# Weight differences of a seven-product scheme: made and split once, and read back by the later blocks

## The chip, the cores and the metric

The kernel runs on one core of a Trainium2 chip. The metric is the device time of one execution, in microseconds (us). The engines are TensorE (PE, with its weight loads shown as PEld), VectorE (DVE), ScalarE (ACT), GpSimd (POOL) and SyncE (SP), which issues most of the DMA transfers.

## The reference

A windowed attention gives 2304 tokens of 512 features. A small network (three products, their maximum, an output product) changes each token's features. Then follows a mixture of 8 experts, in which every token goes through every expert, weighted by a gate that is balanced over 8 rounds:

```python
for e in range(E):                      # E = 8
    h = np.maximum(x @ w1[e], 0.0)      # [2304, 512] @ [512, 1024]
    ye = h @ w2[e]                      # [2304, 1024] @ [1024, 512]
    out += P[:, e:e + 1] * ye
```

The change is in the mixture, in the product with `w2[e]`, "the second product".

## The kernel before

**Splits.** A product in full precision is made of three products of the type fp32r. Each operand X is split into a high part (`hi`: ACT casts X) and a low part (`lo`: X - hi, on POOL or DVE); the three are hi*hi, hi*lo and lo*hi (`PASS`, line 344). The helper `split` (lines 66 to 69) issues the cast (L68) and the subtraction (L69). All casts of all splits carry line 68, all subtractions line 69, so the profile is read by tile names: `wa` (pieces of w1), `wb` and `wt` (pieces of w2), `hop` and `h` (pieces of the hidden values).

**Seven products for eight.** A product of two matrices cut into 2x2 quarters is made of seven quarter products with sums of quarters (Winograd's form of Strassen's scheme). For the second product, with the quarters b11, b12, b21, b22 of a pair of row blocks of w2, the weights are B11, B21, B22 and four differences: T1 = b12 - b11, T2 = b22 - T1, T3 = b22 - b12, T4 = b21 - T2. On the side of the hidden values the sums are S1 to S4.

**Blocks.** The 2304 tokens go in three blocks of 768, each as two halves of 384.

**The first block** (lines 773 to 916) has 32 stages: 8 experts times 4 pairs of 128-wide pieces of the hidden layer. Only the first product uses the seven-product scheme here (matmuls at L788); the second one is done plainly, by `Before.tile` (L740), one stage behind. A stage fetches two raw weight tiles two stages ahead (`fetch_w2`, L527), makes the sums of w1's quarters on DVE (`sums_w2`, L537), splits A1, S12, S34 and A2 for the next stage (`split_w2`: ACT, POOL) and writes each split to a DRAM tensor `wsd` (L557), which the later blocks read. The raw tiles' part of w2 is split whole by `split_out` into `wb`. ACT, DVE and PE run in the order in which the code is written; the orders of POOL's and SP's work are chosen by the scheduler. In stages 0 to 5 the balancing of the gate (`sinkhorn`) is woven in: `next(gate, None)` issues a few small DVE steps or one small matmul (L717). PSUM banks `p` and `q` change roles: the copy of `u2` out of the bank (ACT, L861) must be done before S3's product adds to the same bank.

**The two later blocks** (lines 1034 to 1130) have 16 passes, one for each block and expert. A pass has two halves. The first half makes the hidden values with the first product (L1066, 168 matmuls of 384 columns), with weights read from `wsd` (L563). The second half makes the second product by the seven-product scheme: 28 units u = 7 products x 4 pairs, 9 matmuls of 256 columns each (L998, 252 matmuls). Class `Second` prepares it. `sums` (L950 to L955) makes T1 to T4 on DVE, four subtractions a pair, in place in the raw tile. `weight(u)` splits one weight (ACT cast, POOL subtraction) into a tile `wt`. `mix` (L972, L974) and `rows(u)` (L983 for S4, then the split into `hop`: ACT cast, DVE subtraction) make the other operand. `ready(k)` moves a finished product out of PSUM (L1011, L1016, L1025, L1027). In the second half the code has, for each unit,

```python
sec.product(u)
if u % NPAIR == NPAIR - 1: sec.ready(u // NPAIR)
if 2 * NPAIR <= u + 6 < len(units): sec.rows(u + 6)
if 3 * NPAIR <= u + 10 < len(units): sec.weight(u + 10)
```

so that a unit's `hop` is prepared six units ahead and its `wt` ten.

Of the kernel before, what the change touches and what calls it, by code (L numbers as in the profile page):

```python
# [9 lines left out]
F32 = mybir.dt.float32  # L10
F32R = mybir.dt.float32r
U32 = mybir.dt.uint32
AF = mybir.ActivationFunctionType
ALU = mybir.AluOpType
# [30 lines left out]
E, F2 = 8, 1024  # L45
P = 128
# [15 lines left out]
NPAIR = NF2 // 2  # L62
# [3 lines left out]
def split(nc, hi, lo, src, sub):  # L66

    nc.scalar.copy(hi, src)  # L68
    sub.tensor_tensor(out=lo, in0=src, in1=hi.bitcast(F32), op=ALU.subtract)  # L69
# [16 lines left out]
def attention_moe(ctx: ExitStack, tc: tile.TileContext, q, k, v, mask, wm1, wg, wm2, out):  # L86
    nc = tc.nc
# [15 lines left out]
    cx_p = tc.alloc_tile_pool(name="cx", bufs=3)  # L103
# [5 lines left out]
    xg_p = tc.alloc_tile_pool(name="xg", bufs=1)  # L109
# [162 lines left out]
    x2d = dram.tile([P, KT, NT], F32, name="x2d")  # L272
    x2s = dram.tile([P, 2, KT, NT], F32, name="x2s")
    x2t = dram.tile([4, P, 2, 2, HT], F32, name="x2t")
    wsd = dram.tile([E * NPAIR, 4, P, 2, 512], F32, name="wsd")
    x2 = {}

# [288 lines left out]
    def split_out(raws, i):  # L566
        t = wb2_p.tile([P, 2, 512], F32R, name="wb2")
        split(nc, t[:, 0], t[:, 1], raws[i][:, 1], nc.gpsimd)
        return t

    def fetch_x(blk, queue):
        xs = []
        for j in range(2):
            t = cx_p.tile([P, KT, HT], F32, name="xh", tag="cx")
            c = (2 * blk + j) * HT
            queue.dma_start(t, x2d[:, :, c:c + HT])
            xs.append(t)
        return xs
# [95 lines left out]
    h1_p.release()  # L674
    ps_g.release()
    wb2_p = tc.alloc_tile_pool(name="wb2", bufs=5, reuse_waits="tile")
    h2_p = tc.alloc_tile_pool(name="h2", bufs=2, reuse_waits="tile")
    cc_p = tc.alloc_tile_pool(name="cc", bufs=2, reuse_waits="tile")
    ac_p = tc.alloc_tile_pool(name="ac", bufs=8, reuse_waits="tile")
    sms_p = tc.alloc_tile_pool(name="sms", bufs=1, reuse_waits="tile")  # L680
    ps_c = tc.alloc_tile_pool(name="ps_c", bufs=1, space=PSUM, reuse_waits="tile")

# [90 lines left out]
    for i, (blk, e, n) in enumerate(stages):  # L773
# [49 lines left out]
        def more_x(name):  # L823
            if not last:
                return
            if name[0] == "B":
                load_x(blk + 1, name)
            else:
                split_x(x_ops[blk + 1], name, later_x, nc.gpsimd)
# [3 lines left out]
        def halves(f, j, c):  # L833
            h = hs[f, j]
            nc.scalar.activation(out=h[:, 0], in_=c, func=AF.Relu)
            nc.vector.scalar_tensor_tensor(
                out=h[:, 1], in0=c, scalar=0.0, in1=h[:, 0].bitcast(F32), op0=ALU.max, op1=ALU.subtract
            )
# [13 lines left out]
        product(q, "A12", "B21", True, True)  # L852
        plus(q, m1)
        halves(0, 0, m1)
        more_x("B21")
        sum_x(last or farther)
        second(1, 0)
# [43 lines left out]
        if i:  # L901
            next(gate, None)
        ws.append(split_out(raws, 1))
        more_x("T3")
        keep_x(3)
        keep_x(4)
# [2 lines left out]
        if i + 2 < len(stages):  # L909
            ahead_w[i + 2] = fetch_w2(*stages[i + 2][1:])  # L910
        before = Before((blk, e, n), hs, ws, po, acc)
    for what in UP:
        load_w2(len(stages) + 1, what)
    for j in (1, 0):
# [1 line left out]
            before.tile(j, t)  # L916


    for pool in (sms_p, ac_p, cc_p, h2_p, wb2_p, xg_p, cx_p, sm_p):
        pool.release()  # L920

    def pool(name, bufs=1):
# [14 lines left out]
    class Second:  # L937


        def __init__(self, blk, e, raws):  # L940
            self.blk, self.e, self.raws = blk, e, raws
            self.r, self.h, self.w, self.m, self.ps, self.t2, self.s2 = {}, {}, {}, {}, {}, {}, {}

        def quarters(self, n):
            return {(f, d): self.raws[n][:, f, d * 256:(d + 1) * 256] for f in range(2) for d in range(2)}

        def sums(self, n, last):
            b, sub = self.quarters(n), partial(nc.vector.tensor_tensor, op=ALU.subtract)
            if last:
                sub(out=b[0, 1], in0=b[1, 1], in1=b[0, 1])  # L950
                sub(out=b[1, 0], in0=b[1, 0], in1=self.t2[n])
            else:
                self.t2[n] = tmp_p.tile([P, 256], F32, name="t2", bufs=3)
                sub(out=b[0, 0], in0=b[0, 1], in1=b[0, 0])
                sub(out=self.t2[n], in0=b[1, 1], in1=b[0, 0])  # L955

        def weight(self, u):
            k, n = units[u]
            name = ORD[k][2]
            b = self.quarters(n)  # L960
            if name == "T2":
                src = self.t2[n]
            else:
                src = b[{"B11": (0, 0), "B21": (1, 0), "T1": (0, 0), "T3": (0, 1), "B22": (1, 1), "T4": (1, 0)}[name]]
            t = wt_p.tile([P, 2, 256], F32R, name=f"wt{k % 3}")
            split(nc, t[:, 0], t[:, 1], src, nc.gpsimd)
            self.w[u] = t

        def mix(self, n):
# [64 lines left out]
    for g in range((NBLK - 1) * E):  # L1034
        blk, e = 1 + g // E, g % E
        sec = Second(blk, e, outs.pop(g))
        for n0 in range(0, NPAIR, 2):
# [61 lines left out]
            for k in both:  # L1099
                product(k, 1, "S1", "T1", True)  # L1100
                keep(k, 1, "m1")
                sec.rows(n0 + k)
                sec.sums(n0 + k, False)
            later("S12")
            for k in both:
                product(k, 0, "S3", "T3", False)
                plus(k, 0, "m1", 1, 1)
                sec.sums(n0 + k, True)
            for k in both:
                product(k, 1, "S4", "B22", False)  # L1110
                plus(k, 1, "u2", 0, 1)
# [90 lines left out]
```

## Time and profile before

| what | value |
|---|---|
| median of 3 runs | 1986.23 us (1984.38 to 1986.75) |
| the profiled execution | 1987.47 us, span 1985.7 us, mean granted clock 0.992 |
| PE busy | 1905.0 us (96%) |
| DVE, ACT, POOL busy | 1290.7, 991.6, 837.5 us |
| attention, small network | 0 to about 428 us |
| first block | about 428 to 934 us, 32 stages |
| later blocks | about 934 to 1981 us, 16 passes of 65.5 us (64.7 for expert 0) |

The profiled execution's span runs from its first to its last instruction; its time is 1.8 us longer. Busy time of PE is that of modelled, overlapping matmuls, so what a stretch loses is read from the time between two marks in it, against the number of matmuls between them.

### The profile page before, as it was taken

How to read it: one execution, taken by the hardware profiler on the slowest of the kernel's cores; microseconds unless marked ns; L12 is line 12 of the kernel's file. 1: busy time of each engine (PE TensorE's matmuls, PEld its weight loads, DVE VectorE, ACT ScalarE, POOL GpSimd, SP SyncE). 2: the span in 40 equal slices, each digit the busy share in tenths (PEclk: the TensorE clock that was granted, in tenths of full speed). 3: DMA queues.
4: the chain of work that ended last, by engine and by line, in shares of the span. 5: the costliest groups of instructions: out<-in, count | busy, mean ns of one | idle time of the engine just before them, and what ended most of it. 6: DMA issues, size and time to landing. Idle time of an engine off the chain costs nothing.

```text
span 1985.7 us, 35177 instructions
## 1 busy us (share of the span) xinstructions
PE 1905.0 (96%) x12873; PEld 1800.2 (91%) x12873; DVE 1290.7 (65%) x2361; ACT 991.6 (50%) x2523; POOL 837.5 (42%) x795
## 2 busy tenths in 40 slices
PE   7889999999999999999999999999999999999998
PEld 6789999998889899998999999998999899989998
DVE  7983333437554444444877787778777877787778
ACT  5654453434434444443654565455645565556554
POOL 5673333434444464444433343234423442344233
PEclk7999999999999999999999999999999999999999
DMA  8644445354555575557455344534763346334530
GB/s 266 227 170 160 161 140 196 101 185 175 190 183 190 184 270 187 188 186 279 155 163 160 114 149 152 170 110 146 268 204 116 130 149 191 117 118 149 192 117 33
DMA packets 134861, 334.61 MB, mean 169 GB/s; under 512 B 12705, under 2 KB 58401, under 8 KB 133153
## 3 DMA queue, kind: packets, MB, share of 16 engines
q1 hardware_dynamic: 132000, 328.43, 48.8%
q10 hardware_dynamic: 2688, 3.93, 0.6%
q8 instruction: 102, 1.67, 0.3%
q14 instruction: 71, 0.57, 0.1%
HBM read 246.86 MB, written 85.46 MB: 167 GB/s over the span
## 4 chain that ended last, share of the span: by engine, by line
PE 66%; DVE 20%; ACT 7%; issue 4%; DMA 2%; SPq 0%; POOL 0%; ACTq 0%; DVEq 0%; POOLq 0%
PE po L740 12%; PE po L998 11%; PE ps L379 9%; PE po L1066 9%; DVE hop L69 6%; PE p L788 6%; PE q L788 5%; PE p L1066 4%; PE q L1066 4%; ACT hop L68 3%; PE ps L399 3%; DVE r L983 2%; DVE r L972 2%; ACT wt L68 2%; DVE s L974 1%
## 5 line engine op out<-in xcount | busy, mean ns | idle before, releaser
L998 PE MATMUL po<-wt,hop 128*128 128x256 f32 x4032 | 528.9, 287 | 38.9 <-ACT hop L68 17.2
L998 PEld LDWEIGHTS po<-wt,hop 128*128 128x128 f32 x4032 | 494.9, 191 | 72.3 <-DVE hop L69 28.6
L69 POOL TENSOR_TENSOR wt<-raw,wt 128x256 fp32r<-128x256 f32 x384 | 344.5, 919 | 432.1 <-ACT wt L68 428.1
L69 DVE TENSOR_TENSOR hop<-r,hop 128x384 fp32r<-128x384 f32 x384 | 249.9, 677 | 186.1 <-ACT hop L68 186.1
L740 PE MATMUL po<-wb,h 128*128 128x512 f32 x1152 | 294.5, 392 | 0.2 <-POOL wb L69 0.2
L68 ACT CAST hop<-r 128x384 fp32r<-128x384 f32 x384 | 190.7, 513 | 127.7 <-DVE r L983 127.7
L379 PE MATMUL ps<-xt,wa 128*128 128x288 f32 x1728 | 242.7, 299 | 5.3 <-DVE h L69 3.1
L740 PEld LDWEIGHTS po<-wb,h 128*128 128x128 f32 x1152 | 213.9, 188 | 33.7 <-POOL wb L69 0.7
L379 PEld LDWEIGHTS ps<-xt,wa 128*128 128x128 f32 x1728 | 233.2, 190 | 8.5 <-DVE h L69 3.6
L69 POOL TENSOR_TENSOR wa<-raw,wa 128x512 fp32r<-128x512 f32 x112 | 134.2, 1203 | 170.9 <-ACT wa L68 165.0
L1080 ACT ACTIVATE r<-r 128x384 f32<-128x384 f32 x192 | 100.8, 525 | 170.1 <-DVE r L1079 170.1
L1066 PE MATMUL po<-xT,wa 128*128 128x384 f32 x768 | 157.1, 339 | 0.0
L68 ACT CAST wt<-raw 128x256 fp32r<-128x256 f32 x384 | 155.0, 404 | 0.0
L69 POOL TENSOR_TENSOR wt<-t,wt 128x256 fp32r<-128x256 f32 x64 | 46.8, 740 | 220.7 <-ACT wt L68 220.7
L1066 PEld LDWEIGHTS po<-xT,wa 128*128 128x128 f32 x768 | 135.6, 188 | 2.0
L69 POOL TENSOR_TENSOR wa<-sums,wa 128x512 fp32r<-128x512 f32 x64 | 83.0, 1318 | 93.4 <-ACT wa L68 93.4
L1066 PE MATMUL po<-xB,wa 128*128 128x384 f32 x576 | 116.9, 338 | 0.0
L69 POOL TENSOR_TENSOR wb<-raw,wb 128x512 fp32r<-128x512 f32 x64 | 85.4, 1334 | 59.4 <-ACT wb L68 59.1
L972 DVE TENSOR_TENSOR r<-r,r 128x384 f32<-128x384 f32 x128 | 101.4, 792 | 2.2
L1066 PEld LDWEIGHTS po<-xB,wa 128*128 128x128 f32 x576 | 102.5, 188 | 0.0
L1066 PE MATMUL p<-xT,wa 128*128 128x384 f32 x384 | 79.7, 342 | 3.0 <-DVE r L1079 3.0
L788 PE MATMUL q<-xT,wa 128*128 128x384 f32 x384 | 78.2, 339 | 0.0
(187 smaller groups left out, 3072.0 us busy)
## 6 DMA issues: line engine op xcount, KB each, us to landing
wa<-wsd SPq DMA_DIRECT2D x192, 512.0 KB, 4.4
wsd<-wa SPq DMA_DIRECT2D x96, 512.0 KB, 2.7
raw<-in_wm SPq DMA_DIRECT2D x64, 512.0 KB, 3.6
raw<-in_wm SPq DMA_DIRECT2D x128, 256.0 KB, 2.9
wa<-wsd SPq DMA_DIRECT2D x64, 256.0 KB, 4.5
cx<-in_wm SPq DMA_DIRECT2D x12, 1024.0 KB, 7.1
raw<-wm1f SPq DMA_DIRECT2D x24, 512.0 KB, 3.4
qt<-in_q SPq DMA_DIRECT2D x16, 576.0 KB, 6.1
```

Of the source, the lines that this page charges most:

```text
L68: nc.scalar.copy(hi, src)
L69: sub.tensor_tensor(out=lo, in0=src, in1=hi.bitcast(F32), op=ALU.subtract)
L379: nc.tensor.matmul(ps, w[:, wi, kk], xt[:, xi, kk, n0:n0 + HB], start=(n == 0), stop=(n == 3 * KT - 1),)
L399: nc.tensor.matmul(ps, wo[f][:, wi, d2 * P:(d2 + 1) * P], hs[f][:, hi, a * HB:(a + 1) * HB], start=(f == 0 and n == 0), stop=(f == NF1 - 1 ...
L740: nc.tensor.matmul(po, self.hs[f, j][:, hi, t * P:(t + 1) * P], self.ws[f][:, wi], start=(n + f + k == 0), stop=(n == NPAIR - 1 and f == 1 ...
L788: nc.tensor.matmul(ps, wo[w][:, wi, kk], xo[x][:, xi, kk], start=(first and k == 0), stop=True if k == 5 else False, skip_group_check=not ...
L972: nc.vector.tensor_tensor(out=r[o, n], in0=r[x, n], in1=r[y, n], op=op)
L974: nc.vector.tensor_tensor(out=self.s2[n], in0=r[(1, 1), n], in1=r[(0, 0), n], op=ALU.subtract)
L983: nc.vector.tensor_tensor(out=r[(1, 0), n], in0=r[(1, 0), n], in1=self.s2[n], op=ALU.subtract)
L998: nc.tensor.matmul(self.ps[side, t][:, 0:256], h[:, hi, t * P:(t + 1) * P], w[:, wi], start=(first and i == 0), stop=(n == NPAIR - 1 and i ...
L1066: nc.tensor.matmul(ps[k][side], wo[k][w][:, wi, kk], xo[x][:, xi, kk], start=(first and c == 0), stop=c == 5, skip_group_check=not first,)
L1080: nc.scalar.activation(out=r, in_=r, func=AF.Relu)
```

## The change

The first block now makes T1 to T4 too, splits them and writes the splits to a new DRAM tensor `wtd`; the later blocks load them from there. B11, B21 and B22 are split in the later blocks as before.

- `sums_out`, at the end of each stage: four DVE subtractions on the two raw tiles into a tile `ts` (one buffer).
- `keep_out`, in the next stage behind `halves(0, 0, m1)`: two splits of 512 columns (ACT, POOL) into tiles `tw`, and four DMA writes of 256 KB on SP's queue. For the last stage it stands behind the loop.
- In `Second`, `sums` is gone, and `weight(u)` of a T weight is one DMA load of 256 KB on SP's queue into the same `wt` buffers, in the places where the splits were.
- `ts` and `tw` have a new pool; the pools `cc` and `ac` have 1 and 6 buffers for 2 and 8.

```diff
+    wtd = dram.tile([E * NPAIR, 4, P, 2, 256], F32, name="wtd")
...
+    def sums_out(raws):
+
+        s = wt_p.tile([P, 4, 256], F32, name="ts", bufs=1)
+        (b11, b12), (b21, b22) = ((r[:, 1, 0:256], r[:, 1, 256:512]) for r in raws)
+        for o, x, y in ((0, b12, b11), (1, b22, s[:, 0]), (2, b22, b12), (3, b21, s[:, 1])):
+            nc.vector.tensor_tensor(out=s[:, o], in0=x, in1=y, op=ALU.subtract)
+        return s
+
+    def keep_out(i, s):
+        for o in (0, 2):
+            t = wt_p.tile([P, 2, 512], F32R, name="tw")
+            split(nc, t[:, 0], t[:, 1], s[:, o:o + 2].rearrange("p o n -> p (o n)"), nc.gpsimd)
+            for k in range(2):
+                nc.sync.dma_start(wtd[i, o + k], t[:, :, k * 256:(k + 1) * 256].bitcast(F32))
...
+    wt_p = tc.alloc_tile_pool(name="wto", bufs=2, reuse_waits="tile")
     h2_p = tc.alloc_tile_pool(name="h2", bufs=2, reuse_waits="tile")
-    cc_p = tc.alloc_tile_pool(name="cc", bufs=2, reuse_waits="tile")
-    ac_p = tc.alloc_tile_pool(name="ac", bufs=8, reuse_waits="tile")
+    cc_p = tc.alloc_tile_pool(name="cc", bufs=1, reuse_waits="tile")
+    ac_p = tc.alloc_tile_pool(name="ac", bufs=6, reuse_waits="tile")
...
         halves(0, 0, m1)
+        if i:
+            keep_out(i - 1, ts)
         more_x("B21")
...
         ws.append(split_out(raws, 1))
+        ts = sums_out(raws)
         more_x("T3")
...
+    keep_out(len(stages) - 1, ts)
...
-        def sums(self, n, last):
-            b, sub = self.quarters(n), partial(nc.vector.tensor_tensor, op=ALU.subtract)
...
         def weight(self, u):
             k, n = units[u]
             name = ORD[k][2]
-            b = self.quarters(n)
-            if name == "T2":
-                src = self.t2[n]
+            t = wt_p.tile([P, 2, 256], F32R, name=f"wt{k % 3}")
+            if name[0] == "T":
+                nc.sync.dma_start(t.bitcast(F32), wtd[self.e * NPAIR + n, int(name[1]) - 1])
             else:
-                src = b[{"B11": (0, 0), "B21": (1, 0), "T1": (0, 0), "T3": (0, 1), "B22": (1, 1), "T4": (1, 0)}[name]]
-            t = wt_p.tile([P, 2, 256], F32R, name=f"wt{k % 3}")
-            split(nc, t[:, 0], t[:, 1], src, nc.gpsimd)
+                f, d = int(name[1]) - 1, int(name[2]) - 1
+                split(nc, t[:, 0], t[:, 1], self.raws[n][:, f, d * 256:(d + 1) * 256], nc.gpsimd)
             self.w[u] = t
...
                 sec.rows(n0 + k)
-                sec.sums(n0 + k, False)
...
                 plus(k, 0, "m1", 1, 1)
-                sec.sums(n0 + k, True)
```

## Rows read from the trace of the kernel before

**Rows 1.** Page, part 1: busy us, share of the span, instructions
```profile
PE 1905.0 (96%) x12873; PEld 1800.2 (91%) x12873; DVE 1290.7 (65%) x2361; ACT 991.6 (50%) x2523; POOL 837.5 (42%) x795
```

**Rows 2.** Windows (length; busy PE, PEld, DVE, ACT, POOL; clock; DMA share; GB/s): block, pass, half
```profile
430.00:937.00 507.00, 504.58 (x2523) 453.78 (x2522) 250.88 (x476) 211.22 (x431) 242.96 (x196) 1.00 0.57 203
1003.00:1068.50 65.50, 62.83 (x422) 60.26 (x421) 50.73 (x94) 36.02 (x93) 24.50 (x28) 1.00 0.46 145
1029.20:1064.60 35.40, 32.91 (x254) 30.80 (x253) 29.98 (x51) 19.22 (x53) 16.25 (x18) 1.00 0.27 88
```

**Rows 3.** Chain that ended last, in order of time: start us, us, what
```profile
1029.28 8.65 PE po L998 x72
...
1064.68 1.06 PE q L1066 x6
...
1094.78 8.64 PE po L998 x72
```

**Rows 4.** Timeline of PE: start us, us, instruction, idle before and releaser
```profile
1026.82 1.32 PE L1066 MATMUL p<-xT,wa 128*128 128x384 f32 x6 [0.19 <-DVE r L1079]
...
1044.66 9.73 PE L998 MATMUL po<-wt,hop 128*128 128x256 f32 x79 [0.69 <-DVE hop L69]
...
1056.80 1.69 PE L998 MATMUL po<-wt,hop 128*128 128x256 f32 x9 [0.51 <-ACT hop L68]
```

**Rows 5.** Timeline of DVE in the same pass
```profile
1024.16 0.41 DVE L954 TENSOR_TENSOR raw<-raw 128x256 f32<-128x256 f32 x1
...
1043.53 5.52 DVE L69 TENSOR_TENSOR hop<-r,hop 128x384 fp32r<-128x384 f32 x7
1048.97 0.55 DVE L983 TENSOR_TENSOR r<-r,s 128x384 f32<-128x384 f32 x1
...
1050.65 1.10 DVE L983 TENSOR_TENSOR r<-r,s 128x384 f32<-128x384 f32 x1
...
1052.86 1.09 DVE L983 TENSOR_TENSOR r<-r,s 128x384 f32<-128x384 f32 x1
```

**Rows 6.** Groups by line and form: busy us, mean ns, idle us before, releasers
```profile
L69 POOL TENSOR_TENSOR wt<-raw,wt 128x256 fp32r<-128x256 f32 x384 | 344.5, 919 | 432.1 <-ACT wt L68 428.1 <-DMA wa<-wsd 3.7 <-POOL wt L69 0.4
...
L68 ACT CAST wt<-raw 128x256 fp32r<-128x256 f32 x384 | 155.0, 404 | 0.0
```

**Rows 7.** Timeline of DVE, first block, at a stage's start
```profile
471.97 0.55 DVE L841 TENSOR_TENSOR m<-p,m 128x384 f32<-128x384 f32 x1
...
476.93 0.42 DVE L537 TENSOR_TENSOR sums<-raw 128x256 f32<-128x256 f32 x1
...
478.05 0.42 DVE L537 TENSOR_TENSOR sums<-raw,sums 128x256 f32<-128x256 f32 x1
```

**Rows 8.** Timeline of POOL in the pass of rows 3 to 5
```profile
1038.46 8.77 POOL L69 TENSOR_TENSOR wt<-raw,wt 128x256 fp32r<-128x256 f32 x9 [1.35 <-ACT wt L68]
1050.53 0.81 POOL L69 TENSOR_TENSOR wt<-raw,wt 128x256 fp32r<-128x256 f32 x1 [3.30 <-ACT wt L68]
```

**Rows 9.** DMA issues: KB each, median us from issue to landing
```profile
raw<-in_wm SPq DMA_DIRECT2D x64, 512.0 KB, 3.6
raw<-in_wm SPq DMA_DIRECT2D x128, 256.0 KB, 2.9
```

**Rows 10.** Timeline of PE at that stage's start
```profile
472.57 0.39 PE L717 MATMUL p<-sms,ones 128*128 128x8 f32 x2
```

**Rows 11.** Timeline of SP in a later stage of the first block
```profile
708.33 0.34 SPq L527 DMA_DIRECT2D raw<-in_wm  x1
```

**Rows 12.** Timeline of ACT, that stage and the next
```profile
710.45 0.60 ACT L68 CAST wa<-raw 128x512 fp32r<-128x512 f32 x1
...
727.76 0.62 ACT L68 CAST wa<-raw 128x512 fp32r<-128x512 f32 x1 [1.60 <-DMA raw<-in_wm]
```

**Rows 13.** Timeline of PE, third product of that stage's first bank
```profile
715.39 1.21 PE L788 MATMUL p<-xT,wa 128*128 128x384 f32 x6
```

**Rows 14.** Windows in the first block, columns as in rows 2
```profile
718.00:734.00 16.00, 16.00 (x82) 14.51 (x82) 7.95 (x12) 8.47 (x18) 12.00 (x11) 1.00 0.95 336
```

More of the change, by code (lines that the diff above doesn't have):

```diff
@@ L916, in attention_moe @@
             before.tile(j, t)
-    for pool in (sms_p, ac_p, cc_p, h2_p, wb2_p, xg_p, cx_p, sm_p):
+    for pool in (sms_p, ac_p, cc_p, h2_p, wt_p, wb2_p, xg_p, cx_p, sm_p):
         pool.release()
@@ L941, in __init__ @@
             self.blk, self.e, self.raws = blk, e, raws
-            self.r, self.h, self.w, self.m, self.ps, self.t2, self.s2 = {}, {}, {}, {}, {}, {}, {}
-        def quarters(self, n):
-            return {(f, d): self.raws[n][:, f, d * 256:(d + 1) * 256] for f in range(2) for d in range(2)}
-        def sums(self, n, last):
-            b, sub = self.quarters(n), partial(nc.vector.tensor_tensor, op=ALU.subtract)
[L949 to L955, printed above, removed]
+            self.r, self.h, self.w, self.m, self.ps, self.s2 = {}, {}, {}, {}, {}, {}
         def weight(self, u):
```

## The prediction

> **What bounds the kernel now.** I read the page's totals first: PE is busy for 96% of the span [rows 1], so only PE's waits can be won, and where they lie decides. The windows by stretch say where: in the first block PE is busy for 504.58 of 507 us [rows 2], so nothing is to be won there and any new wait is a loss. A pass of the later blocks lasts 65.5 us from one mark of the chain to the next (1029.28 to 1094.78) [rows 3]. PE's work in it is 168 matmuls at 1.06/6 = 0.176 us and 252 at 8.65/72 = 0.120 us, 29.6 + 30.2 = 59.8 us [rows 3]. So a pass loses 5.7 us, the 16 passes about 16 x 5.7 = 91 us. (Two passes, those of expert 0, lose 0.8 us less; this goes into the rounding.) The split of a pass: its second half takes 1064.68 - 1029.28 = 35.4 us for 30.2 us of work, 5.2 us lost; its first half takes 30.1 us for 29.6.
>
> PE's timeline names what those waits end on: a `plus` of the first half on DVE, then `hop` on DVE and on ACT [rows 4], and four more like them, two of which end on `ready`. No wait ends on POOL's `wt` or on a load: the weights themselves are in time, and it is the other operand that is late. Why it is late stands in DVE's timeline. `sums` lies in the first half's DVE work [rows 5]. From 1043.53 seven `hop` subtractions take 5.52 us, 0.79 each, without a gap: DVE is behind. From 1048.97 each of the units 20 to 23 goes DVE (L983), ACT, DVE, one after the other; L983 takes 0.55 us the first time and 1.10 us after that, and the round is 1052.86 - 1050.65 = 2.21 us, twice PE's 9 x 0.120 = 1.08 us a unit.
>
> **What the change removes from a pass.** 16 subtractions of `sums` (DVE), 16 of 28 casts of `wt` (ACT, mean 0.404 us) and 16 of 28 subtractions of `wt` (POOL, mean 0.919 us) [rows 6].
> - DVE, directly: alone, such a subtraction takes (478.05 - 476.93)/3 = 0.37 us [rows 7]. The eight of the pass's second pair of stages stand in front of the second half's preparation: 8 x 0.37 = 3.0 us earlier.
> - DVE, indirectly: POOL worked from 1038.46 to 1047.23 on nine `wt` [rows 8], beside the seven slow `hop`. The one L983 that ran alone took 0.55 us; the next ran from 1050.65 beside POOL's `wt` from 1050.53 and took 1.10 [rows 5, 8]. Most of those `wt` are T weights and go. A 384-column subtraction alone is then some 0.5 us, by 0.37 x 384/256 = 0.55 and by L983: the seven `hop` gain 7 x (0.79 - 0.5) = 2.0 us, three L983 gain 3 x 0.55 = 1.65 us.
> - Sum for DVE: 3.0 + 2.0 + 1.65 = 6.7 us a pass, more than the 5.7 us that PE loses. ACT gains 16 x 0.404 = 6.5 us, of which twelve casts lie between the `hop` casts.
>
> A rule bears on the second of these. The Trainium skill, "SBUF — State Buffer", section "Who interferes with whom", says that a DVE instruction with two SBUF inputs contends with a GpSimd instruction that reads SBUF. The pair 0.55 and 1.10 us agrees. If L983 stayed at 1.10 us with POOL idle, the rounds of 2.21 us would start earlier but stay, and I estimate 1 us of the gain lost in a pass: 16 us more in the time.
>
> What is late next? I laid the instructions of the second half out again in their order, with 0.37 us for 256 and 0.5 us for 384 columns on DVE and PE at 1.08 us a unit. Counted from unit 0's start, `rows(12)` is done at 7.6 us; `ready(1)` waits for unit 7, to 8.6, and ends at 11.3; `rows(13)` to `rows(19)` end at 16.6, so unit 20's L983 starts there instead of at 1048.97 - 1029.28 = 19.7 [rows 3, 5]. Four rounds of 3 x 0.5 us bring DVE to 22.6, where PE wants unit 20 at 21.6 and has had it since 18.1. `ready(4)` then ends at 25.7, and unit 25's `hop` at 26.1, where PE wants it at 27.0: this is the tightest place, with 0.9 us. So PE's own work is the bound. I keep 0.5 us a pass for hand-overs that this doesn't show: gain 16 x (5.7 - 0.5) = 83 us. Bounds: nothing kept, 91 us; 1.7 us kept in each pass (a third of what is lost now), 64 us.
>
> **What it adds to a pass.** 16 loads of 256 KB on SP's queue; such loads land after 2.9 us [rows 9]. Twelve fall into the second half, where the DMA engines are busy for 0.27 of the time [rows 2]. `weight(u+10)` is issued behind unit u, its buffer's last reader was unit u-2, so 9 units, 9.7 us, cover 2.9 us. On SP nothing that waits for long stands before them: `wa` loads belong to the first half, the eight raw loads come at unit 18. Cost 0; if the cover went, up to 3 us a pass.
>
> **What it adds to the first block, 32 stages.** Per stage four DVE subtractions (1.5 us alone), two ACT casts and two POOL subtractions of 512 columns, 1 MB of writes. By the window POOL is busy for 242.96/32 = 7.6 of 15.8 us, DVE for 7.8, ACT for 6.6, the DMA engines for 0.57 at 203 GB/s [rows 2]; 1 MB in 15.8 us is 66 GB/s more. There is room on average; three places are not average.
> - Sinkhorn stages: behind the gate's steps on DVE comes `plus` at 471.97, and PE's L717, which reuses the bank that `plus` reads, starts only behind it, at 472.57 [rows 7, 10]. `sums_out` goes between: 478.47 - 476.93 = 1.54 us [rows 7], nothing hides it. Three such stage starts lose 1.54 us in full, one, which has 0.7 us of slack, half: 5.4 us.
> - Raw tiles: they come free only after `sums_out`. The second one's fetch, issued at 708.33 [rows 11], and with it now the first one's comes up to 3.1 us later (twice 1.54, if DVE runs beside POOL), as I take it 1.3. It lands 3.6 us after that [rows 9]. The A1 cast (710.45 [rows 12]) waits for it, behind it the copy of `u2`, and S3's product at 715.39 needs that copy [rows 13]. 708.33 + 1.3 + 3.6 + 0.6 (cast) + 0.5 (copy) = 714.3: hidden by 1.1 us. With 3.1 it is 0.7 us late, in some 28 stages 20 us. I take 0 and keep 20.
> - Two stages around 718 to 750: the DMA engines are busy for 0.95 at 336 GB/s and POOL for 12 of 16 us [rows 14], and the A1 cast waits for its raw tile already (1.60 us) [rows 12]. Later fetches and 66 GB/s more: 2 us each, 4 us; bounds 0 and 10.
> - At the block's end the extra writes meet the loads for the next block: 1.5 us, bounds 0 and 5.
> The smaller pools cost nothing: a `cc` tile's last reader is long done a stage later, and only six `ac` tiles are in use.
>
> Sum: -83 + 5.4 + 4 + 1.5 = -72 us. Against the profiled execution's 1987.5 us that is 1915.5; this execution lies 1.2 us above the median of 1986.2, so 1914 us.
>
> **The rivals.**
> - *The first block follows the raw tiles.* The chain fetch, A1 cast, `u2` copy, S3 sets every stage's length. For it: the cover is only about 1 us. Against it: DVE is busy for only 7.8 of a stage's 15.8 us [rows 2], so that `sums_out` should mostly run at once. At the 0.7 us late of the upper bound and 0.5 for a landing among the new writes, 32 x 1.2 = 38 us less gain: 1952 us.
> - *The waits move instead of vanishing.* T loads come late behind other transfers, or `ready` and `rows` on DVE hold PE at another unit: half of the gain stays, 1914 + 42 = 1956 us. For it: PE's order is fixed and the margin at unit 25 is 0.9 us. Against it: the DMA share of 0.27.
> - *Slower.* SP takes its work in the scheduler's order. If the raw fetch stands behind the four new writes of a stage, which wait for POOL, it comes some 6 us later than now; with landing, cast and copy that is 708.33 + 6 + 4.7 = 719.0 where PE wants 715.39 [rows 11, 13], 3.6 us a stage: 31 x 3.6 = 112 us lost against 83 won, 2015 us. It decides from 83/32 = 2.6 us a stage. Against it: the writes belong to the differences of the stage before and are ready in mid-stage, long before the fetch.
> - *Nothing happens.* The differences are loaded, but `hop` is late for reasons of its own. Against it: DVE's work falls by more than PE's loss. With the first block's losses of 5 to 11 us 1991 to 1997 us.
>
> **How the numbers follow.** Forecast 0.70 (1895 to 1940 us), first block by raw tiles 0.11, waits moved 0.09, slower 0.07, nothing 0.03. The range is to hold 8 in 10: the forecast's own and the near parts of the first two rivals, 1895 to 1953 us; its low end is 91 won and 5 lost, less some 5 us for waits of the first half that I count as PE's own work. A difference of 0.2% (4 us) is about what a measurement can tell from no change. Faster 0.90, same 0.02, slower 0.08.
>
> **What would show it.** Right: passes of about 60.3 us between the same marks; L983 at about 0.55 us in the mean; PE's idle before L998 nearly gone; `wt` casts 192 instead of 448; the first block's waits grown at L717 (by about 5 us) and around 718 to 750 only. Wrong: an A1 cast that waits for its raw tile in most stages, with stages of 17 us instead of 15.8; L998 waiting for a DMA `wt<-wtd`; or passes above 62 us with L983 still at 1.1 us.

## The result, and the profile after

The changed kernel takes 1922.33 us (median of four runs, 1920.43 to 1922.93), the kernel before beside it 1985.74 us: a ratio of 0.9679 with a 95% interval of 0.9663 to 0.9696, 63.4 us less. The prediction was 1914 us with a range of 1895 to 1953. The profiled execution took 1922.74 us with a span of 1921.0; before, the span was 1985.7.

In the changed kernel some lines have other numbers: L983 is now L990, L998 L1005, L1066 L1073, L717 L734, L788 L805, L836 L853, L841 L858, L537 L538. `sums_out` is L577, the T weights' loads are L970, the halves of a split L68 and L69 as before.

The page of the changed kernel: busy time by engine, then groups (busy us, mean ns | idle before them and its releaser) and DMA issues (KB each, us to landing).

```profile
PE 1868.8 (97%) x12873; PEld 1799.0 (94%) x12873; DVE 1235.1 (64%) x2233; ACT 965.6 (50%) x2331; POOL 713.7 (37%) x603
...
L1005 PE MATMUL po<-wt,hop 128*128 128x256 f32 x4032 | 491.4, 284 | 3.6 <-DVE hop L69 3.5
...
L69 POOL TENSOR_TENSOR wt<-raw,wt 128x256 fp32r<-128x256 f32 x192 | 170.3, 909 | 782.5 <-ACT wt L68 770.3
L69 DVE TENSOR_TENSOR hop<-r,hop 128x384 fp32r<-128x384 f32 x384 | 224.5, 611 | 229.0 <-ACT hop L68 229.0
...
wt<-wtd SPq DMA_DIRECT2D x256, 256.0 KB, 3.5
...
raw<-in_wm SPq DMA_DIRECT2D x64, 512.0 KB, 4.1
...
raw<-in_wm SPq DMA_DIRECT2D x128, 256.0 KB, 5.0
```

Of POOL's 448 `wt` subtractions 192 are left: half of the form that [rows 6] show (384), and none of the 64 of T2, which have a form of their own. PE's idle time ahead of the second product's matmuls is 3.6 us in the whole execution. And a raw tile of 256 KB takes 5.0 us to land where it took 2.9 [rows 9].

The chain of the changed kernel, second halves of three passes (start us, us, what), then the window of one pass (length; busy PE, PEld, DVE, ACT, POOL; granted clock; DMA share; GB/s):

```profile
1040.46 30.41 PE po L1005 x252
...
1100.44 30.41 PE po L1005 x252
...
1160.42 30.42 PE po L1005 x252
```
```profile
1100.44:1160.42 59.98, 59.98 (x422) 59.83 (x422) 40.89 (x77) 32.18 (x77) 10.65 (x12) 1.00 0.71 229
```

Where the chain of before had several pieces to a half [rows 3], the 252 matmuls are now one piece. From mark to mark a pass takes 59.98 us instead of 65.5, and PE is busy in all of it. POOL's work fell from 24.5 to 10.65 us and the DMA share rose from 0.46 to 0.71 [rows 2].

DVE in the second half of the pass from 1160.42:

```profile
1174.93 1.87 DVE L69 TENSOR_TENSOR hop<-r,hop 128x384 fp32r<-128x384 f32 x2 [0.16 <-ACT hop L68]
1176.72 1.09 DVE L990 TENSOR_TENSOR r<-r,s 128x384 f32<-128x384 f32 x1
...
1178.94 0.55 DVE L990 TENSOR_TENSOR r<-r,s 128x384 f32<-128x384 f32 x1
...
1180.61 0.55 DVE L990 TENSOR_TENSOR r<-r,s 128x384 f32<-128x384 f32 x1
```

Unit 20's L990 starts 16.3 us into the half (predicted 16.6, before 19.7) and is the only one of the four that still runs beside POOL, at 1.09 us. The other three take 0.55 us. It is so in all 16 passes: 16 of the 64 L990 are slow, and the mean is 0.69 us (0.96 before).

**The ledger of the two spans.** The later blocks took 1046.95 us before (934.34 to 1981.29 on the chain) and take 965.35 us (951.02 to 1916.37): 81.6 us won, 83 predicted. Fifteen passes are within 0.3 us of 59.98 (59.71 to 60.25), but one is not. It is the pass that ends the middle block and loads the next one's operands. PE's timeline there, and windows with the columns above:

```profile
1400.45 13.10 PE L1005 MATMUL po<-wt,hop 128*128 128x256 f32 x108
1417.03 19.85 PE L1005 MATMUL po<-wt,hop 128*128 128x256 f32 x144 [3.48 <-DVE hop L69]
...
1466.29 3.98 PE L1005 MATMUL po<-wt,hop 128*128 128x256 f32 x32
```
```profile
1410.00:1415.00 5.00, 3.55 (x30) 3.35 (x28) 4.15 (x8) 2.95 (x9) 1.27 (x2) 1.00 1.04 386
1415.00:1420.00 5.00, 2.97 (x14) 3.00 (x15) 2.93 (x4) 1.62 (x5) 2.54 (x3) 0.55 0.97 345
1420.00:1425.00 5.00, 5.00 (x35) 5.00 (x35) 1.16 (x3) 1.50 (x4) 0.00 (x0) 0.76 0.92 285
```

This pass takes 65.84 us. Unit 12 waits for 3.48 us, then the granted clock has a mean of 0.55 in one stretch and 0.76 in the next, between its two levels (1.2 and 2.4 GHz), and the 144 matmuls take 19.85 us instead of 17.3 (144 x 0.120): 3.48 + 2.5 = 6.0 us, against 65.84 - 59.98 = 5.9. The releaser that the profile names, `hop`, isn't the cause. DVE works in the code's order, and counted by it unit 12's own `hop` was done at 1408.3; the one that ends at 1416.97 is for unit 19. What unit 12 waits for is its T1 load. It is issued at 1406.77, 6.3 us into the half (1.1 us in a usual pass), and lands 10.1 us later, at 1416.9, with the DMA engines at a share of 1.0; in a usual pass it lands after 4.0 us. The view of the tile `wt` from 1395 to 1425:

```profile
DMA to landing us min/median/max: 5.1/6.5/10.1
```

In other runs of the same place the profile names the load `wt<-wtd` itself as the releaser.

The first block and the change-over behind it, from its first stage to the first product of the later blocks, grew by 14.95 us (predicted 10.9). The attention part ahead of it ended 1.73 us later; in the kernels below, with the same code there, this point lies between 424.8 and 430.7 us, so I make nothing of it. The tail took 0.2 us more. 81.6 - 14.95 - 1.73 - 0.2 = 64.7 us, the difference of the spans.

This is the ledger of one execution, and two of its entries vary. In the profiled executions of the eight kernels whose first block is the changed kernel's, that block with the change-over takes 522.1 to 526.9 us; here it is 522.55, near the low end (507.60 before). The pass of 65.84 us takes 62.05, 63.6 and 64.2 us in three kernels below that change nothing in it, so 65.84 is the longest that was seen of it.

PE's waits in the first block, in the order of time:

```profile
458.51 0.39 PE L734 MATMUL q<-sms,ones 128*128 128x8 f32 x2 [0.47 <-DVE m L858]
...
476.38 0.39 PE L734 MATMUL p<-sms,ones 128*128 128x8 f32 x2 [1.54 <-DVE m L858]
...
494.24 0.39 PE L734 MATMUL q<-sms,ones 128*128 128x8 f32 x2 [1.54 <-DVE m L858]
...
512.12 0.39 PE L734 MATMUL p<-sms,ones 128*128 128x8 f32 x2 [1.54 <-DVE m L858]
...
574.99 1.60 PE L805 MATMUL p<-xB,wa 128*128 128x384 f32 x6 [2.04 <-DVE h L853]
576.39 2.76 PE L757 MATMUL po<-wb,h 128*128 128x512 f32 x6
```

The four at L734 are the predicted ones. The wait at 574.99 was 0.60 us before; there DVE also adds the products of an expert that is done to `acc` (L775, L778), which is called the expert's "take" below. Behind this wait the clock falls too (0.66 from 575 to 580): six matmuls of L757 take 2.76 us where the groups around them take 1.54, and the two stages take 35.22 us instead of 32.08. What sets the end of the waits there, around 690 and in the crowded stretch is on the chain:

```profile
558.50 4.45 DMA raw<-in_wm
...
685.19 2.08 DVE ts L577 x3
...
687.39 4.38 DMA raw<-in_wm
...
720.69 5.30 DMA raw<-in_wm
...
729.19 1.52 DVE sums L538
...
738.44 3.58 DMA raw<-in_wm
...
756.44 5.50 DMA raw<-in_wm
```

So in these few places the first block does follow the raw tiles: `sums_out` reads the last of a tile, its fetch is issued, and it lands 3.6 to 5.5 us later.

### The profile page after: what moved, and what is told of

It reads as the page before. It is cut to its first block, busy times and chain, and to the rows that moved or that the text cites. A ratio compares the mean times of both kernels' runs of the same rounds, so it can differ in the third digit from the quotient of the medians.

```text
span 1921.0 us, 35293 instructions
## 1 busy us (share of the span) xinstructions
PE 1868.8 (97%) x12873; PEld 1799.0 (94%) x12873; DVE 1235.1 (64%) x2233; ACT 965.6 (50%) x2331; POOL 713.7 (37%) x603
## 4 chain that ended last, share of the span: by engine, by line
PE 82%; DVE 8%; DMA 4%; ACT 2%; issue 2%; POOL 1%; SPq 0%; ACTq 0%; DVEq 0%; POOLq 0%
PE po L1005 24%; PE po L1073 12%; PE po L757 10%; PE ps L380 10%; PE q L1073 6%; PE p L1073 6%; PE p L805 5%; PE q L805 4%; PE ps L400 3%; DMA raw<-in_wm 1%; DVE ts L577 1%; DMA x2s<-xg 1%; DVE h L853 1%; DMA qt<-in_q 1%; DMA cx<-in_wm 1%
## 5 line engine op out<-in xcount | busy, mean ns | idle before, releaser
L1005 PE MATMUL po<-wt,hop 128*128 128x256 f32 x4032 | 491.4, 284 | 3.6 <-DVE hop L69 3.5
L1005 PEld LDWEIGHTS po<-wt,hop 128*128 128x128 f32 x4032 | 488.7, 193 | 5.7 <-ACT wt L68 3.7
L69 POOL TENSOR_TENSOR wt<-raw,wt 128x256 fp32r<-128x256 f32 x192 | 170.3, 909 | 782.5 <-ACT wt L68 770.3
L69 DVE TENSOR_TENSOR hop<-r,hop 128x384 fp32r<-128x384 f32 x384 | 224.5, 611 | 229.0 <-ACT hop L68 229.0
L757 PE MATMUL po<-wb,h 128*128 128x512 f32 x1152 | 295.9, 393 | 0.9 <-POOL wb L69 0.9
L757 PEld LDWEIGHTS po<-wb,h 128*128 128x128 f32 x1152 | 214.7, 189 | 34.9 <-POOL wb L69 1.7
L68 ACT CAST hop<-r 128x384 fp32r<-128x384 f32 x384 | 187.9, 514 | 97.6 <-DVE r L990 72.0
L69 POOL TENSOR_TENSOR wa<-raw,wa 128x512 fp32r<-128x512 f32 x112 | 135.2, 1210 | 75.4 <-ACT wa L68 74.9
L1073 PE MATMUL po<-xT,wa 128*128 128x384 f32 x768 | 155.9, 338 | 0.0
L1073 PEld LDWEIGHTS po<-xT,wa 128*128 128x128 f32 x768 | 136.7, 188 | 0.0
L69 POOL TENSOR_TENSOR tw<-ts,tw 128x512 fp32r<-128x512 f32 x64 | 84.1, 1335 | 95.9 <-DVE h L853 61.0
L1073 PE MATMUL po<-xB,wa 128*128 128x384 f32 x576 | 116.9, 338 | 0.0
L69 POOL TENSOR_TENSOR wa<-sums,wa 128x512 fp32r<-128x512 f32 x64 | 86.8, 1375 | 56.9 <-ACT wa L68 34.7
L69 POOL TENSOR_TENSOR wb<-raw,wb 128x512 fp32r<-128x512 f32 x64 | 95.0, 1485 | 26.0 <-ACT wb L68 25.5
L1073 PEld LDWEIGHTS po<-xB,wa 128*128 128x128 f32 x576 | 102.5, 188 | 0.0
L979 DVE TENSOR_TENSOR r<-r,r 128x384 f32<-128x384 f32 x128 | 93.1, 727 | 2.2
L68 ACT CAST wa<-raw 128x512 fp32r<-128x512 f32 x112 | 61.6, 555 | 58.2 <-DMA raw<-in_wm 31.2
L538 DVE TENSOR_TENSOR sums<-raw 128x256 f32<-128x256 f32 x64 | 41.4, 649 | 72.6 <-DMA raw<-in_wm 72.3
L1018 ACT COPY mm<-po 128x256 f32<-128x256 f32 x144 | 47.0, 377 | 71.9 <-PE po L1005 71.9
```

The lines of the kernel that those rows point to most:

```text
L538: nc.vector.tensor_tensor(out=s[:, o], in0=x, in1=y, op=op)
L757: nc.tensor.matmul(po, self.hs[f, j][:, hi, t * P:(t + 1) * P], self.ws[f][:, wi], start=(n + f + k == 0), stop=(n == NPAIR - 1 and f == 1 ...
L979: nc.vector.tensor_tensor(out=r[o, n], in0=r[x, n], in1=r[y, n], op=op)
L1005: nc.tensor.matmul(self.ps[side, t][:, 0:256], h[:, hi, t * P:(t + 1) * P], w[:, wi], start=(first and i == 0), stop=(n == NPAIR - 1 and i ...
L1018: nc.scalar.copy(m, ps)
L1073: nc.tensor.matmul(ps[k][side], wo[k][w][:, wi, kk], xo[x][:, xi, kk], start=(first and c == 0), stop=c == 5, skip_group_check=not first,)
```

## The experiments

Each run is compared with the changed kernel's 1922.3 us. Unless a median is given, a kernel's time is that of one execution, which can lie some us from its median (1916.88 to 1926.95 in one kernel's five executions). So the usual passes, nearly all of which repeat within 0.1 us, carry the verdicts; the pass that changes the block does not repeat. "A pass" is the distance of two marks on the chain away from the change of blocks.

**The differences alone** (e1_no_diff): the kernel before, without `sums`, its T weights split from the plain quarters.

```diff
-            if name == "T2":
-                src = self.t2[n]
-            else:
-                src = b[{"B11": (0, 0), "B21": (1, 0), "T1": (0, 0), "T3": (0, 1), "B22": (1, 1), "T4": (1, 0)}[name]]
+            if True:
+                src = b[{"T2": (1, 1), "B11": (0, 0), "B21": (1, 0), "T1": (0, 0), "T3": (0, 1), "B22": (1, 1), "T4": (1, 0)}[name]]
...
-                sec.sums(n0 + k, False)
...
-                sec.sums(n0 + k, True)
```

> The kernel before, with the differences of the later blocks left out (the T weights are split from plain quarters): only the DVE subtractions go, all splits and the first block stay. Theory (DVE was late by three things: the differences, 3.0 us a pass, and two kinds of subtraction slowed beside POOL, 3.65 us): L983 stays near 1.1 us, passes of about 62.5 us, 1938 us. Rival 1 (the splits on ACT and POOL alone made hop late, the differences had cover): passes of 65 us, 1980 us. Rival 2 (the differences alone were the cause): passes of 60 us, 1900 us.

1955.04 us. A pass takes 63.46 us, 2.0 less than before, and the 64 subtractions that were L983 are not faster (the view of their line, here L981: ns min/median/max):

```profile
L981 DVE TENSOR_TENSOR r<-r,s x64: 543/1092/1101, 982.0 to 1939.2; 128x384 f32<-128x384 f32 x64
```

**The splits alone** (e2_diff_kept): the changed kernel, with the 16 subtractions of `sums` put back and their results unused.

```diff
+        def sums(self, n, last):
+            b, sub = self.quarters(n), partial(nc.vector.tensor_tensor, op=ALU.subtract)
...
+                sec.sums(n0 + k, False)
...
+                sec.sums(n0 + k, True)
```

> The kernel after, with the DVE subtractions of the later blocks kept and their results unused: only the splits of the T weights are gone. Theory: L990 at about 0.55 us, but DVE is 3.0 us later in a pass: passes of about 62 us, 1922 + 32 = 1954 us. Rival 1 (splits alone): passes of 60 us as in the kernel after, 1922 us. Rival 2 (differences alone): passes of 65 us, 2002 us.

1930.30 us, a pass 60.51 us. The median of the L990 subtraction is 0.55 us here as well:

```profile
L1003 DVE TENSOR_TENSOR r<-r,s x64: 550/553/1090, 998.6 to 1915.5; 128x384 f32<-128x384 f32 x64
```

So by itself the end of the splits is worth 65.50 - 60.51 = 5.0 us a pass and the end of the differences 2.0. Once the splits are gone, the differences are worth 60.51 - 59.98 = 0.5 us. By halves: without the differences the first half takes 29.57 us (30.10 before) and the second 33.91 (35.40); without the splits 30.11 and 30.41. So the splits cost the second half alone, and the last 0.5 us that the differences cost lies in the first half. My theory, that the direct and the indirect part are of equal size and add, missed both runs.

**Which half of a split** (e3_casts_kept, e8_splits_kept, e9_memset): the changed kernel with dummy work into a tile that nobody reads, in place of the 16 splits a pass that went: ACT's cast alone; the whole split; the cast and, on POOL, a memset of about the subtraction's length.

```diff
+                spare = tmp_p.tile([P, 256], F32R, name="spare", bufs=1)
+                nc.scalar.copy(spare, self.raws[n][:, 1, 256:512])
```
```diff
+                spare = tmp_p.tile([P, 2, 256], F32R, name="spare", bufs=4)
+                split(nc, spare[:, 0], spare[:, 1], self.raws[n][:, 1, 256:512], nc.gpsimd)
```
```diff
+                spare = tmp_p.tile([P, 960], F32R, name="spare", bufs=2)
+                nc.scalar.copy(spare[:, 0:256], self.raws[n][:, 1, 256:512])
+                nc.gpsimd.memset(spare.bitcast(F32), 0.0)
```

> The kernel after, with the 16 ACT casts of each pass kept (into an unused tile): no differences on DVE, no POOL subtractions of T weights. Theory (POOL beside DVE is what the splits cost, ACT's casts have cover): L990 at about 0.55 us, passes of 60 to 60.5 us, 1922 to 1928 us. Rival (ACT's casts between the hop casts made hop late): passes of 62 us or more, at least 1955 us.

> The kernel after, with the 16 whole splits of T weights of each pass kept, ACT cast and POOL subtraction, into an unused tile. Theory (POOL's subtractions slow DVE's two-input subtractions beside them, which is most of what the change wins): L990 back at about 1.1 us, passes of 63 to 63.5 us as without the differences alone, 1972 us. Rival (POOL's work costs only where a weight waits for it): passes stay at 60 us, 1925 us.

> As the run before, but POOL writes 960 zeros a partition where it would subtract: as busy (about 0.9 us each), without reading SBUF. Theory (two reads meet): L990 stays at 0.55 us and passes at 60 to 60.5 us, 1925 us. Rival (any work of POOL slows DVE): L990 near 1.1 us and passes of 63 us, 1972 us.

1924.92, 1972.96 and 1921.74 us. The window of one pass of each, in this order:

```profile
1103.79:1163.84 60.05, 60.04 (x422) 59.84 (x422) 41.15 (x77) 36.63 (x93) 10.58 (x12) 1.00 0.70 230
```
```profile
1074.88:1138.37 63.49, 61.83 (x421) 60.23 (x421) 45.61 (x78) 36.67 (x93) 24.57 (x28) 1.00 0.67 214
```
```profile
1102.66:1162.69 60.03, 60.03 (x422) 59.83 (x422) 41.14 (x77) 36.93 (x93) 24.67 (x29) 1.00 0.71 228
```

The second and the third differ in what POOL does in the same 24.6 us: subtract, which reads SBUF, or write zeros (of more columns, to take as long). The pass is 3.5 us longer with the subtractions, and DVE's busy time 4.5 us more for the same instructions. On DVE's own line (ns min/median/max) the subtraction beside them takes twice its time, beside the memsets not:

```profile
L992 DVE TENSOR_TENSOR r<-r,s x64: 542/1092/1107, 999.3 to 1956.6; 128x384 f32<-128x384 f32 x64
```
```profile
L993 DVE TENSOR_TENSOR r<-r,s x64: 549/551/1092, 999.3 to 1906.8; 128x384 f32<-128x384 f32 x64
```

The rule of the Trainium skill, "SBUF — State Buffer", section "Who interferes with whom", that such a DVE instruction contends with a GpSimd instruction that reads SBUF and not with one that only writes it, agrees with both lines: 1.092 and 0.551 us. Each of the 64 can be laid beside POOL's work. With the subtractions, 48 run beside one and are slow, and the 16 that run alone are fast. With the memsets, 48 run beside a memset and are fast, and the 16 beside a subtraction of B22, which stayed, are slow. ACT's casts cost next to nothing (60.05 us against 59.98). The run with the whole splits also equals the first experiment's pass, 63.49 and 63.46 us: with POOL's work back, the loads and the missing differences make no other difference.

**Where `sums_out` stands** (e5_early_sinkhorn, e11_mid_stage): ahead of the seventh product in the Sinkhorn stages; and, in every stage, behind the next tile's `sums_w2` with `keep_out` at the stage's own end.

```diff
+        if 1 <= i <= 4:
+            ts = sums_out(raws)
...
-        ts = sums_out(raws)
+        if not 1 <= i <= 4:
+            ts = sums_out(raws)
```
```diff
-        if i:
-            keep_out(i - 1, ts)
...
+        ts = sums_out(raws)
...
-        ts = sums_out(raws)
...
+        keep_out(i, ts)
...
-    keep_out(len(stages) - 1, ts)
```

> The kernel after, with the four subtractions of the first block moved ahead of the seventh product in stages 1 to 4 alone. Theory (they stand between the gate's steps and the stage's first plus, for which L734 waits): the four long stages go back from 16.8 and 17.9 us to some 16.1 and 16.5, 4.8 us less, 1917.5 us. Rival (DMA writes or late raw tiles make these stages long): they keep their length, 1922 us.

> The kernel after, with the four subtractions of the first block right behind those for the first product's weights, in mid-stage, and the splits and writes at the same stage's end: the same work and the same bytes, elsewhere. Theory (a DVE that is full at a stage's end and raw tiles freed late cost the first block its 15 us): stages of 15.6 us but for the gate's, 10 to 14 us less, 1908 to 1912 us. Rival (the writes and POOL's new work cost it): 1920 to 1924 us.

1919.65 and 1922.49 us: no gain that can be told. In the first of them the four Sinkhorn stages take 70.89 us (455.0 to 525.9) where the changed kernel takes 70.4. The waits at L734 are gone, and others have come two products later. PE's timeline, and DVE's ahead of the second of these waits:

```profile
473.75 1.32 PE L805 MATMUL p<-xB,wa 128*128 128x384 f32 x6 [1.42 <-DVE h L853]
...
492.09 1.33 PE L805 MATMUL q<-xB,wa 128*128 128x384 f32 x6 [1.63 <-DVE h L853]
```
```profile
487.49 1.44 DVE L577 TENSOR_TENSOR ts<-raw 128x256 f32<-128x256 f32 x1
488.97 0.84 DVE L577 TENSOR_TENSOR ts<-raw,ts 128x256 f32<-128x256 f32 x1
489.74 1.49 DVE L577 TENSOR_TENSOR ts<-raw 128x256 f32<-128x256 f32 x1
```

There the subtractions run beside POOL's (which are without a gap from 484.18 to 490.95) and take up to 1.49 us each instead of 0.42. Further from the gate's chain they are beside POOL; away from POOL they are in the gate's chain. The second run brought the four stages to 77.6 us (451.4 to 529.0), with a wait at L734 at nearly every half of a stage, and left the wait behind the expert's take at 2.01 us; what it won in the stage behind 690 (16.15 us for 17.12) and at the block's end (24.24 for 25.73) is less than that. My theory that the place of `sums_out` is what costs the 15 us fell with both: neither place that was tried is better.

**The gate's steps** (e14_gate_thin): fewer steps of the gate's chain in the stages that DVE's wait lies in.

```diff
         def window():
-            if i:
+            if 1 <= i <= 3:
                 next(gate, None)
                 next(gate, None)
```

> The changed kernel, but the gate's steps inside the stages are given only to the stages 1 to 3 of the first block and not to those after them, so DVE has less to do in some of the early stages. Theory (DVE is full in the early stages, so the added subtractions come out as PE's waits; the stage with the take of the second expert's weights loses 3.1 us to this): those waits shrink, total about 1919 us. Rival (the waits come from a chain that the gate's steps don't lengthen, or the gate's end is only late elsewhere): 1922 us or more.

1922.68 us. Two of the four waits at L734 are gone; in their place stand four on ACT, of which two rows of PE's timeline:

```profile
498.00 1.32 PE L805 MATMUL p<-xT,wa 128*128 128x384 f32 x6 [0.58 <-ACT u L880]
...
514.67 1.32 PE L805 MATMUL q<-xT,wa 128*128 128x384 f32 x6 [0.54 <-ACT u L880]
```

The five stages from 454 take 84.7 us instead of 86.0, the two behind them 32.9 instead of 31.2, and the wait behind the take is still 2.02 us. The rival holds: the chain only ends later.

**The pass of 65.84 us** (e6_x_later, e13_x_on_act, e16_x_on_pool): the loads of the next block's operands (6 x 384 KB and 4 x 768 KB, 5.4 MB) put behind units 10 and 18 in the code, on SP as before; the same on ACT's queue; and on POOL's, behind the units 2 to 20 in the code, one by one. The second diff shows only the line in which it differs from the first.

```diff
-                if turn_x and k:
-                    load_x(blk + 1, x)
...
+            if turn_x and u in (10, 18):
+                for x in ("B11", "B21", "T2", "T1") if u == 10 else ("T3", "B22", "T4"):
+                    load_x(blk + 1, x)
```
```diff
+                    load_x(blk + 1, x, nc.scalar)
```
```diff
+        X_AT = {2: "B11", 5: "B21", 8: "T2", 11: "T1", 14: "T3", 17: "B22", 20: "T4"}
...
+            if turn_x and u in X_AT:
+                load_x(blk + 1, X_AT[u], nc.gpsimd)
```

> The kernel after, with the loads of the last block's tokens, 5.4 MB at the end of the eighth pass, issued behind units 10 and 18 instead of in the first half. Theory (they stand in the DMA queues before the T1 weights, so unit 12 waits): the eighth pass goes from 65.8 to about 60 us, 1922 - 5.5 = 1916.5 us. Rival (unit 12 waits for something else, such as hop): 1922 us.

> The changed kernel, but in the pass that ends an expert (the eighth), the seven loads of the next block's attention operands are issued on ACT's queue behind units 10 and 18 instead of by SP ahead of the T1 loads. Theory (the 5.85 us that this pass takes beyond the others are T1 loads that land late behind the operand loads, and the lower clock after that wait): the eighth pass falls from 65.8 to about 60 us, unit 12 no longer waits, its 144 matmuls take about 17.3 instead of 19.85 us, total about 1916.5 us. Rival (the wait is on DVE's hop, as the profile names it, or the loads only push the next block's start back by as much): the pass stays near 65.8 us or the next block starts as much later, total 1922 us.

> The changed kernel, but in the pass that ends an expert the seven operands of the next block are loaded on POOL's queue, one at a time behind the units 2, 5, 8, 11, 14, 17 and 20. It tells apart what took the place of unit 12's wait when ACT issued them (there the run was 1926.45 us and the pass 67.1 us, with ACT's copy of mm late by up to 6.3 us behind the issues). Theory (the burst ahead of the T1 loads costs the pass 5.85 us, and ACT lost it again only because its casts and copies stood behind the issues): on POOL, which is busy for a fifth of the time there, the pass takes some 60 to 61 us and the total is about 1917 us. Rival (the pass needs more bytes in its second half than the DMA engines move, wherever they are issued): the T1 loads stay late or the next block starts late, pass and first half of the next together still some 5 us above the others, total 1922 us or more.

The first gave 1926.05 us and did not do what it was to do: SP issued the operands still from 1392.94 to 1410.56, ahead of the T1 loads at 1411.42, because the scheduler sets SP's order. But there PE's wait of 2.75 us at unit 12 has the releaser `wt<-wtd`, the load.

On ACT's queue the loads did go out behind the T1 loads, from 1412.34 on. The T1 load of unit 12, issued at 1403.64, landed after 3.9 us, and unit 12 no longer waits: this shows that the operands ahead of it made it late. Yet the pass takes 67.1 us and the run 1926.45. PE's timeline and ACT's (ACTq is its queue of DMA issues):

```profile
1402.35 22.23 PE L1005 MATMUL po<-wt,hop 128*128 128x256 f32 x180
1425.27 6.76 PE L1005 MATMUL po<-wt,hop 128*128 128x256 f32 x39 [0.68 <-ACT mm L1018]
...
1434.70 5.34 PE L1005 MATMUL po<-wt,hop 128*128 128x256 f32 x27 [0.99 <-ACT hop L68]
```
```profile
1412.77 2.44 ACTq L620 DMA_DIRECT2D xB<-x2s  x3
1417.46 1.86 ACTq L615 DMA_DIRECT2D xT<-x2t  x2
1419.36 0.93 ACT L1018 COPY mm<-po 128x256 f32<-128x256 f32 x3 [6.29 <-DMA xB<-x2s]
```

ACT's copy of `mm` stood behind the issues for 6.29 us, and PE waited for it and for the casts behind it. The wait had moved to another engine.

On POOL's queue the profiled execution took 1916.88 us and its pass 62.7 us. But this edit did not do what it was to do either. POOL's order is the scheduler's too: POOL issued all ten loads by 1398.5, around the end of the first half, several of them right behind PE's last use of the tile (`<-PE po L1073`), and all of them before the first T1 load. PE's timeline, POOL's with the first and the last of the loads, and the chain's piece for the T1 load:

```profile
1397.49 13.10 PE L1005 MATMUL po<-wt,hop 128*128 128x256 f32 x108
1413.32 17.51 PE L1005 MATMUL po<-wt,hop 128*128 128x256 f32 x144 [2.73 <-DMA wt<-wtd]
```
```profile
1385.29 1.59 POOL L620 DMA_DIRECT2D xB<-x2s  x2 [9.23 <-PE po L1073]
...
1397.96 0.55 POOL L615 DMA_DIRECT2D xT<-x2t  x1 [0.68 <-PE po L1073]
```
```profile
1398.78 14.40 DMA wt<-wtd
```

Unit 12's load took 14.40 us to land, and unit 12 waits for it as in the others, 2.73 us, but the clock stays and the 144 matmuls take 17.51 us. From 1390 to 1430 the DMA share is 1.01 to 1.05 in every 5 us (347 to 415 GB/s); on ACT's queue, with the operands later, it is 0.73 to 0.89 up to 1415. So this run tests neither the theory nor its rival: the operands stood ahead of the T1 loads once more. Nor is its 62.7 us a gain, since the pass takes 62.05 to 65.84 us in kernels that leave it as it is. Over five runs the median is 1921.14 us (1916.88 to 1926.95), the ratio to before 0.968 (0.9666 to 0.9694): not told apart from the changed kernel.

**Both edits** (e15_both): operands on ACT's queue and the thinner gate.

> The changed kernel with both edits: operand loads on ACT's queue behind units 10 and 18, and the gate's steps in the stages 1 to 3 only. If both theories hold the gains add, since they lie in different blocks: about 1913.5 us. If only the loads' order matters 1916.5, if only the gate's 1919, if neither 1922 us.

1921.62 us over five runs (1918.93 to 1924.83), ratio 0.9672 (0.9658 to 0.9686), again not told apart from the changed kernel. Unit 12 doesn't wait here either, and the pass takes 65.2 us. No version here beats it by more than the measurement can tell.

## Why the prediction was right, and its sizes

*The pass.* The chain of reasons held: DVE was late, the change takes work from it, PE's own work becomes the bound. I took 59.8 us of PE work, kept 0.5 for hand-overs, and had 60.3; it is 59.98. The prediction's tightest place, unit 25, brought no wait. One sign that I had named did not come: L983 was to take about 0.55 us in the mean and takes 0.69, because unit 20's still runs beside POOL in every pass. It didn't matter, since PE doesn't wait there.

*The terms of DVE's sum* were off, though their sum sufficed. The direct term, 3.0 us for the differences, all of it in the second half, is worth 2.0 alone (1.5 of it in the second half) and 0.5 with the splits gone. The indirect term, 3.65 us by the `hop` and the L983 beside POOL, is worth 5.0 alone. They overlap, since a pass can give back only the 5.5 us that PE lost. POOL's reads were the main cause of the loss, and the differences the smaller one. That POOL's subtractions, not ACT's casts, do it is shown by the pair of runs with subtraction and memset; that L983 alone is the place of it is not shown, and is unlikely: its four a pass differ by 4 x (0.956 - 0.686) = 1.1 us, while DVE's busy time differs by 4.5 us, so the pass's other DVE instructions shared the slowing.

*The loads.* "Cost 0; if the cover went, up to 3 us a pass" held in fifteen passes and failed in the one where the operands of the next block are loaded. I read the DMA share of 0.27 in an ordinary pass [rows 2] and did not look at this pass by itself. The wait alone lies around the bound of 3 us (3.48, 2.75, 2.73 us in three runs, the first of them above it); the lower clock behind it wasn't in the sum. I had also written that nothing that waits for long stands before the T loads on SP; in this pass the operands do. Against 83 us predicted, 81.6 came, with nothing kept in the ordinary passes and 5.9 lost here.

*The first block.* Sinkhorn stages: 5.4 predicted, 4.8 measured (16.79 + 3 x 17.87 against 16.11 + 16.50 + 16.51 + 16.50), at L717's successor, as said. The crowded stages: 4 predicted for the two from 718 to 750, which lost 2.2; the two behind them, up to 785, which I hadn't named, lost 2.4. The block's end: 1.5, 1.4, but by another cause than I gave: 1.02 us of it is PE's wait for `h` on DVE at 927.52, behind an `h` of 1.52 us and an `xd` of 2.03 us that took 0.56 and 0.95 before, and not a load that meets the writes. So these two numbers came out right in part by luck. Not predicted: 3.1 us in the two stages around 575 and 1.0 behind the fetch at 687. The term that was mis-sized is that of the raw tiles, taken as 0: there the tile's fetch after `sums_out` takes 4.4 us and DVE's `sums_w2` waits for it, rather than ACT's A1 cast, through which I had laid the chain. The rival "the first block follows the raw tiles" is thus true in these places and in the crowded stages, and false in the other stages, which take the same 15.61 us as before. Of the 3.1 us 1.4 are the longer wait, and 1.6 come with the lower clock: the run with the operands on POOL's queue has the same wait there, 2.01 us, a clock of 1.00 behind it, and 33.62 us for the two stages instead of 35.22.

*The total.* The sum gave 1915.5 us for the profiled execution, which took 1922.7. Of these 7.2 us the passes are 1.4 (83 against 81.6): the fifteen usual ones were about 0.32 us shorter each than the 60.3 expected, 4.8 to 5.0 us together, the one of 65.84 us was 5.5 longer, before the sixteen together were 1.0 us shorter than 16 x 65.5, and 0.2 is rounding. The first block is 4.1, the start of the stages 1.7.

What stays open: whether the pass that changes the block could be brought to 60. The run on ACT's queue shows that operands issued behind the T1 loads leave these in time, but there the issues held up ACT's own work. No run had loads that go out as late without holding up an engine: on SP and on POOL the scheduler put them first.

## What to carry to other kernels

When an instruction on DVE has two lengths, look at what POOL does during the long one before counting instructions: taking away a POOL subtraction that nobody waits for was worth more here than taking away the DVE work beside it. A load that is hidden in an ordinary pass has to be looked up again in the pass where the next block's data come in, since there the DMA engines were at a share of 1.0. Work that is moved on an engine that is busy for most of a stage (DVE 14.5 of 17.9 us in the Sinkhorn stages) can bring the same wait elsewhere, as all three experiments on the first block did. And before a run with a load moved in the code is read, its issue times have to be looked up: on SP and on POOL the loads did not go where the code had put them.

## What the runs showed of the hardware that was not expected

Behind waits of the same length PE's granted clock fell in some executions and not in others. After 2.75 us at unit 12 the 144 matmuls took 19.00 us (operands moved in the code on SP), after 2.73 us 17.51 (operands on POOL), after 2.08 us again 19.00 (thin gate), and after 1.88 us 17.67 (`sums_out` early). What decides it, the runs don't show. It makes 1.5 to 2.5 us at each such place, and may be part of the spread of 1916.88 to 1926.95 us over five runs of one kernel.
